# Filling a two-layer gated MLP kernel: where weights are loaded, decoded and where the first convolutions are summed

## Chip, cores and metric

One NeuronCore of a Trainium2 chip. The metric is the device time of one execution, in microseconds. The profile is one execution taken by the hardware profiler; every "row" below is from it.

## What is computed

Inputs are `x` (2 x 4096 x 192), `weight_gen` (2 x 4096 x 8 x 7) and four weight matrices that reach the kernel as 64-bit floats (drawn as float64). The result is 8192 x 192.

```python
w = softmax(weight_gen, axis=-1)                      # 8 heads, 7 taps
x1[b, s, h*24 + g] = sum_k w[b, s, h, k] * x_pad[b, s + k, h*24 + g]   # causal, 6 zeros ahead
x2 = (sigmoid(x1 @ w_gate) * (x1 @ w_val)) @ w_out1   # 192 -> 1536 -> 192
h  = x2 @ w_in2                                       # 192 -> 2048
out = (h * cos(h)) @ w_out2                           # 2048 -> 192
```

## The kernel before

**Tiling.** 8192 tokens are 128 partitions x 64 token columns; a chunk `c` is TC = 4 of those columns, so 512 tokens, and there are NCH = 16 chunks. Every operand of a matmul is split into a high and a low part in fp32r (`split`, line 117: ACT copies the high part, POOL subtracts to get the low part), and three of the four products are summed. Contraction runs over 64 rows, two row halves side by side, so matmuls come in pairs "64x512".

**Steps.** A `Step` (line 505) is one column block of a layer. A layer-1 step has 18 `ph` matmuls (`hidden`, line 422), then on ACT a sigmoid (`gate`, line 527), on DVE the product (`product1`, line 530), on ACT and POOL the two halves `gh` and `gl` (`halves`, lines 565 and 566), and later 10 `po` matmuls (`out_matmuls`, line 437) that sum the output. Layer 1 has 12 steps per chunk. Layer 2 has 8 steps of two blocks each, with a reduction, a Sin and a product in place of the sigmoid.

**Order.** All steps stand in one list (`segments`, line 593): layer 1 of chunks 0 and 1 first, then layer 2 of chunk 0, layer 1 of chunk 2, layer 2 of chunk 1, and so on. I call layer 1 of chunks 0 and 1 the *fill*: steps 0 to 11 and 12 to 23. The order on each engine is written out by hand. Work that belongs to a later step (softmax, taps, weight decode) stands in a list `side` with a due step, and `do_side` (line 614) emits it ahead of that step's matmuls. Each engine runs its instructions in that order.

**Weights.** A weight piece (`Unit`, line 123, and `OutUnit`, line 148) is DMA'd from the SP queue as two 32-bit words per element and decoded to fp32 (`decode`, line 99): ACT scales the high word (line 106) and the low word (line 107), DVE joins them (line 109), DVE puts the sign back (line 113). Layer-2 input pieces are then scaled on ACT (line 141). Then `split` makes the halves: ACT at line 118, POOL at line 120 or 172. There are 18 pieces: 2 of 384 and 16 of 768 elements a partition (`u` names gate/value or layer-2 input, `o` names output weights). In emission order the split of a piece (line 118) stands ahead of the next step's sigmoid.

**Convolution.** Seven taps (`pr`, `acc`). For chunk 0 each product (DVE half of the heads, POOL half) is transposed by TensorE into the same PSUM banks (line 332), which sums them. For chunks 1 and 2 DVE takes 6 of 8 heads and POOL 2, multiplying and adding into `acc` (lines 268, 282, 292); from chunk 3 on DVE has all heads. `acc` is then extended by a copy (line 313) and transposed in two batches of 12 matmuls (`transpose_tiles`, line 369), with `po` matmuls behind each; ACT copies the high parts (line 400), DVE subtracts to the low parts (line 403), 384 wide, into all slots of `xT`. `first_input` (line 405) does the same for chunk 0 in ten pairs of copy and subtract (lines 416, 417). For layer 2, `finish1` (line 461) fills one slot and a half itself and the others with three SBUF-to-SBUF DMAs.

**Queues.** All DMAs are issued by SP. There are eight completion semaphores; a DMA issue waits until the earlier DMA on its semaphore has landed.

Of the kernel before, what the change touches and what calls it, by code (L numbers as in the profile page):

```python
# [29 lines left out]
def dyn_conv_glu_cos_mlp(  # L30
# [15 lines left out]
    P = 128  # L46
# [15 lines left out]
    NS = NQ + 1  # L62
# [59 lines left out]
    class Unit:  # L122
# [13 lines left out]
        def ops(self):  # L136
# [11 lines left out]
    class OutUnit:  # L148
# [15 lines left out]
        def ops(self):  # L164
# [3 lines left out]
            self.t = wpool.tile([P, JG, 2 * D], F32R, name="outu", tag=self.name)  # L168
            f = f.rearrange("p (j d) -> p j d", j=JG)
# [33 lines left out]
    def load_group(g, tiles, tag):  # L203
# [3 lines left out]
        nc.sync.dma_start(  # L207
# [32 lines left out]
    def load_x(c):  # L240
# [8 lines left out]
        if h:  # L249
            for b in range(B):  # L250
                p0 = b * per_batch
                nc.sync.dma_start(
# [393 lines left out]
    with tc.manual_schedule():  # L646
# [53 lines left out]
        for _ in s0:  # L700
            pass
# [138 lines left out]
```

## Time and profile before

| what | value |
|---|---|
| median of 3 runs | 1293.6 us (1292.59 to 1294.15) |
| profiled execution | 1293.17 us |
| its span, first to last instruction | 1291.4 us |
| PE busy in the span | 1236.2 us (96%), 10984 matmuls |
| DVE, ACT, POOL busy | 942.7, 810.9, 736.6 us |
| mean granted TensorE clock | 0.975 of full |

The span is 1.8 us shorter than the execution's time. PE is busy 96% of the whole, but that is a mean over unlike parts: the first 160 us differ from the rest, so the stretches have to be read one at a time. Busy time on PE includes time at half clock, which the granted clock tells (1.0 is 2.4 GHz, 0.5 is 1.2 GHz).

### The profile page before, as it was taken

The page shows a single profiled execution, that of the slowest core. Times are in us where ns is not written, and L with a number is a line of the kernel's source. Part 1 is how long each engine was busy: PE and PEld are TensorE (multiplying, and loading weights), DVE is VectorE, ACT ScalarE, POOL GpSimd, SP SyncE. Part 2 cuts the span into 40 slices and gives each one's busy share as a digit, 9 for nine tenths or more (in the row PEclk, how much of TensorE's full clock was granted, in tenths as well). Part 3 has the DMA queues.
Part 4 walks back from the last instruction along what each step waited for, and adds up shares of the span by engine and source line. Part 5 has one row for each costly group of instructions (what it writes and reads, how often), then busy time and mean ns, then how long its engine had stood idle before and what let it go on. Part 6 is the DMA issues. An engine that isn't in the chain of part 4 may idle for free.

```text
span 1291.4 us, 26697 instructions
## 1 busy us (share of the span) xinstructions
PE 1236.2 (96%) x10984; PEld 1037.2 (80%) x10984; DVE 942.7 (73%) x1323; ACT 810.9 (63%) x1345; POOL 736.6 (57%) x563
## 2 busy tenths in 40 slices
PE   6687799999999999999999999999999999999997
PEld 4465688888888888888888888888888888888885
DVE  6979688777778677777867777786776768673585
ACT  5564584756748475674847567484756748475675
POOL 5778664554646455474746547374654737464473
PEclk7788899999999999999999999999999999999999
DMA  9951010100111100011110001111000111010010
GB/s 213 184 122 55 1 37 13 53 28 32 26 44 26 55 17 22 32 25 44 26 54 18 22 31 26 44 25 48 21 18 32 26 44 26 13 26 14 1 26 26
DMA packets 21066, 51.51 MB, mean 40 GB/s; under 512 B 1876, under 2 KB 6482, under 8 KB 20944
## 3 DMA queue, kind: packets, MB, share of 16 engines
q1 hardware_dynamic: 20944, 49.80, 15.2%
q8 instruction: 86, 1.41, 0.5%
q14 instruction: 36, 0.29, 0.1%
HBM read 30.92 MB, written 6.29 MB: 29 GB/s over the span
## 4 chain that ended last, share of the span: by engine, by line
PE 75%; DVE 6%; ACT 2%; issue 1%; POOL 0%; DVEq 0%; ACTq 0%
PE ph L430 41%; PE po L449 33%; DVE acc L292 2%; DVE wk L530 1%; ACT wk L527 1%; PE pt L377 1%; DVE wk L538 1%; ACT gh L565 1%; DVE va L459 1%; DVE wk L546 1%; DVE wk L555 0%; DVE wk L541 0%; ACT wk L551 0%; POOL gl L566 0%; PE pf L490 0%
## 5 line engine op out<-in xcount | busy, mean ns | idle before, releaser
L566 POOL TENSOR_TENSOR gl<-wk,gh 128x512 fp32r<-128x512 f32 x446 | 606.5, 1365 | 507.2 <-ACT gh L565 385.2
L430 PE MATMUL ph<-xT,unit 64*128 64x512 f32 x5760 | 781.8, 393 | 20.4 <-ACT wk L527 11.0
L430 PEld LDWEIGHTS ph<-xT,unit 64*128 64x128 f32 x5760 | 612.2, 187 | 128.9 <-ACT wk L527 13.6
L449 PE MATMUL po<-gh,outu 64*128 64x512 f32 x2688 | 565.3, 394 | 16.3 <-ACT outu L118 6.4
L449 PE MATMUL po<-gl,outu 64*128 64x512 f32 x1792 | 473.3, 390 | 2.9 <-POOL gl L566 2.8
L449 PEld LDWEIGHTS po<-gh,outu 64*128 64x128 f32 x2688 | 408.4, 186 | 70.2 <-DVE va L459 10.8
L565 ACT ACTIVATE gh<-wk 128x512 fp32r<-128x512 f32 (+1 forms) x450 | 282.8, 629 | 272.4 <-DVE wk L530 216.7
L449 PEld LDWEIGHTS po<-gl,outu 64*128 64x128 f32 x1792 | 324.7, 186 | 34.4 <-POOL gl L566 4.2
L530 DVE TENSOR_TENSOR wk<-ph,wk 128x512 f32<-128x512 f32 x192 | 131.7, 686 | 153.7 <-ACT wk L527 144.7
L555 DVE SCALAR_TENSOR_TENSOR wk<-ph,wk 128x512 f32<-128x512 f32 (+1 forms) x258 | 166.9, 686 | 39.7 <-ACT wk L551 39.7
L551 ACT ACTIVATE wk<-wk,sin_bias 128x512 f32<-128x512 f32 (+1 forms) x258 | 171.4, 714 | 9.7 <-DVE wk L541 3.3
L527 ACT ACTIVATE wk<-ph 128x512 f32<-128x512 f32 x192 | 113.8, 593 | 50.4 <-PE ph L430 49.4
L538 DVE TENSOR_SCALAR wk<-ph 128x512 f32<-128x512 f32 x129 | 87.9, 682 | 66.9 <-PE ph L430 63.6
L292 DVE TENSOR_TENSOR acc<-acc,pr 128x768 f32<-128x768 f32 (+1 forms) x90 | 123.3, 1370 | 0.4
L545 ACT ACTIVATE wk<-ph 128x512 int32<-128x512 f32 x129 | 75.7, 587 | 74.5 <-PE ph L430 73.8
L282 DVE TENSOR_TENSOR pr<-xp,sm 128x768 f32<-128x768 f32 (+1 forms) x90 | 103.2, 1147 | 0.1
L541 DVE SCALAR_TENSOR_TENSOR wk<-wk,ph 128x512 f32<-128x512 f32 x129 | 88.1, 683 | 4.4
L546 DVE TENSOR_TENSOR wk<-wk,ph 128x512 f32<-128x512 int32 x129 | 87.3, 677 | 0.0
L459 DVE TENSOR_TENSOR va<-po,va 128x512 f32<-128x512 f32 x32 | 22.0, 687 | 34.6 <-PE po L449 32.5
L403 DVE TENSOR_TENSOR xT<-pt,xT 128x384 fp32r<-128x384 f32 x60 | 30.6, 552 | 18.1 <-ACT xT L400 18.1
L400 ACT ACTIVATE xT<-pt 128x384 fp32r<-128x384 f32 x60 | 26.2, 488 | 16.6 <-PE pt L377 16.6
L120 POOL TENSOR_TENSOR unit<-wf,unit 128x768 fp32r<-128x768 f32 (+1 forms) x11 | 21.1, 1917 | 19.3 <-ACT unit L118 19.3
(66 smaller groups left out, 566.5 us busy)
## 6 DMA issues: line engine op xcount, KB each, us to landing
xp<-in_x_dram SPq DMA_DIRECT2D x14, 960.0 KB, 4.7
xT<-xT SPq DMA_DIRECT2D x48, 256.0 KB, 3.3
out_dram<-o SPq DMA_DIRECT2D x16, 384.0 KB, 2.3
rawo<-in_moe_w_out_dram SPq DMA_DIRECT2D x7, 768.0 KB, 21.3
raw<-in_moe_w_in_dram SPq DMA_DIRECT2D x8, 384.0 KB, 20.7
raw<-in_moe_w_gate_dram SPq DMA_DIRECT2D x5, 384.0 KB, 15.2
raw<-in_moe_w_val_dram SPq DMA_DIRECT2D x5, 384.0 KB, 15.6
sm<-in_weight_gen_dram SPq DMA_DIRECT2D x5, 336.0 KB, 5.1
```

What stands on the lines that cost most here:

```text
L282: eng.tensor_tensor(out=pr.rearrange("p t (h g) -> p t h g", g=G), in0=xt[:, k:k + TC, a * G:b * G].rearrange("p t (h g) -> p t h g", g=G) ...
L292: eng.tensor_tensor(out=acc[:, :, c], in0=acc[:, :, c], in1=pr, op=ALU.add)
L430: nc.tensor.matmul(ps[i], lhsT=u.t[i * HP:(i + 1) * HP, w, q, c0:c0 + P], rhs=tokens(xt, x, i, q), start=n == 0, stop=n == len(terms) - 1,)
L449: nc.tensor.matmul(po[2 * i + a], lhsT=w[r, d0:d0 + P], rhs=g[r], start=first and g is gh and d0 < D, stop=last and g is gl,)
L527: nc.scalar.activation(out=self.w[0], in_=self.ps[0], func=AF.Sigmoid)
L530: nc.vector.tensor_tensor(out=self.w[0], in0=self.ps[1], in1=self.w[0], op=ALU.mult)
L538: nc.vector.tensor_scalar(out=w, in0=u, scalar1=0.25, scalar2=ROUND_MAGIC, op0=ALU.add, op1=ALU.add)
L546: nc.vector.tensor_tensor(out=w, in0=w.bitcast(I32), in1=u, op=ALU.subtract)
L551: nc.scalar.activation(out=w, in_=w, func=AF.Sin, scale=-SIN_SCALE, bias=sin_bias)
L555: nc.vector.scalar_tensor_tensor(out=w, in0=self.ps[i][:, r], scalar=TWO_PI, in1=w, op0=ALU.mult, op1=ALU.mult)
L565: nc.scalar.activation(out=gh, in_=w, func=AF.Copy)
L566: eng.tensor_tensor(out=gl, in0=w, in1=gh.bitcast(F32), op=ALU.subtract)
```

## The change

- Weight loads: the gate part of a piece goes by SP, the value part by ACT's DMA queue, from the first piece to the last of layer 1; softmax weights and one of the two history blocks of chunk 0's input go by ACT too. The history of chunk 1's input is copied on POOL from chunk 0's tile.
- Decode: ACT uses Prelu with a scale and a slope instead of Copy, so that the sign bit comes out of the shift; the second DVE operation (line 113) is gone.
- A piece's split is put in a list `late` and emitted behind the step's sigmoid, not ahead of it.
- Decodes have new due steps; layer 2's eight DVE decodes all stand at steps 13 to 22.
- Convolutions of chunks 0, 1, 2: DVE multiplies all heads, nothing is added on DVE or POOL, TensorE transposes all seven products into the same banks (16 matmuls each, 8 of them 64 columns of weights wide). One or four warm-up matmuls follow each tap of chunk 0. Chunk 1's input is made one step earlier (AHEAD = 2).
- First two steps: their high-part products are issued ahead of the low-part ones (`mm_high`).
- Inputs of chunks 2 to 15: one batch of 16 transposes; ACT and DVE fill one slot and a half, and three DMAs copy the other slots (`exchange`), as for layer 2.

The diff, cut:

```diff
     def decode(raw, f):
-        nc.scalar.activation(out=f, in_=raw[:, :, 1].bitcast(F32), func=AF.Copy, scale=2.0**-112)
+        nc.scalar.activation(
+            out=f, in_=raw[:, :, 1].bitcast(F32), func=AF.Prelu, scale=2.0**-112, alpha=2.0**32
+        )
         nc.scalar.activation(out=low, in_=low, func=AF.Copy, scale=LOW_SCALE)
         yield
         nc.vector.scalar_tensor_tensor(
             out=fi, in0=fi, scalar=3, in1=low, op0=ALU.logical_shift_left, op1=ALU.bitwise_or
         )
-        yield
-        nc.vector.scalar_tensor_tensor(
-            out=fi, in0=raw[:, :, 1], scalar=1 << 31, in1=fi, op0=ALU.bitwise_and, op1=ALU.bitwise_or
-        )
...
+            late.append(lambda: self.halves(f))
...
-        if h:
+        if c == 1:
+            nc.gpsimd.tensor_copy(out=t[:, 0:h, :], in_=xp[0][:, TC:TC + h, :])
+        elif h:
             for b in range(B):
                 p0 = b * per_batch
-                nc.sync.dma_start(
+                queues[b % 2].dma_start(
...
+    def conv_products(c):
+        big = tpool.tile([P, K - 3, TC, D], F32, name="prs", tag="xA" if c % 2 == 0 else "xB")
+        att[c] = [big[:, k] for k in range(K - 3)] + [product_tile(), product_tile(), acc_tile()]
+        for k, pr in enumerate(att[c]):
+            tap(c, k, pr)
+            yield
...
+    def transposes(p, src, first, end):
+        blocks = [(0, 0)] + [(2, t) for t in range(TC)] + [(0, t) for t in range(1, TC)]
...
+    def split_input(xt, p, fast):
+        for slot in (OWN[0], OTHER[0], OWN[1]) if fast else OWN:
+            high(nc.scalar, xt, p, slot)
+        yield
+        if fast:
+            for slot in OTHER[1:]:
+                high(nc.vector, xt, p, slot)
+        for slot in (OWN[0], *OTHER[:2], OWN[1], OTHER[2]) if fast else OWN:
+            low(xt, p, slot)
+        if not fast:
+            exchange(xt)
...
-        todo += [(s2 + u.j0 - 3, u) for u in units2] + [(s2 + o.j0 // 2, o) for o in outs2]
+        todo[n1:] = [(seg_start[1, 1] + 1 + i * (J1 - 1) // 8, u) for i, (_, u) in enumerate(todo[n1:])]
...
+        for k, _ in enumerate(first_input()):
+            if k in (3, 5):
+                next(decoding)
+                run(late)
+            if k == 2:
+                units1[3].load(act, 1)
+                units1[4].load(act, 1)
+            if k == K:
+                units1[5].load(act, 1)
+                units1[6].load(sp, 0)
+                units1[6].load(act, 1)
+                outs1[2].load(sp)
+            else:
+                warm_up(1 if k < K - 1 else 4)
+        for st in steps[:2]:
+            st.mm_high()
...
                 st.gate()
+                run(late)
                 pending.append(st.product1)
```

How the order of instructions moves, at three places. First ACT in step 17 of the fill, the decode of a layer-2 piece. Names: `raw` loaded words, `wf` decoded piece, `unit` its high half, `wk` the sigmoid's output, `gh` the high half of the step's result. Before (the like place, ahead of the sigmoid of step 19):

```order
L565 ACTIVATE gh<-wk 128x512 [waits DVE_49]
L106 ACTIVATE wf<-rawo 128x768 [waits DMAHW7_49]
L107 ACTIVATE rawo<-rawo 128x768
L141 ACTIVATE wf<-wf 128x768 [waits DVE_49]
L118 ACTIVATE unit<-wf 128x768 [waits Activation_49]
L527 ACTIVATE wk<-ph 128x512 [waits PE_49,Pool_49]
L565 ACTIVATE gh<-wk 128x512 [waits DVE_49]
```

After:

```order
L547 ACTIVATE gh<-wk 128x512 [waits DVE_49]
L146 ACTIVATE wf<-wf 128x768 [waits DVE_49]
L109 ACTIVATE wf<-rawo 128x768 [waits DMAHW5_49,Activation_49]
L112 ACTIVATE rawo<-rawo 128x768
L509 ACTIVATE wk<-ph 128x512 [waits PE_49]
L119 ACTIVATE unit<-wf 128x768 [waits Activation_49]
L547 ACTIVATE gh<-wk 128x512 [waits DVE_49]
```

The split of the piece (L118, now L119) has moved from ahead of the sigmoid to behind it.

Second, ACT from the transposed first input on, after the change; before, the loads stood on SP and row L106 followed the copies of `xT` directly:

```order
L349 ACTIVATE xT<-pt 64x4x64 x4
L136 DMA raw<-in_moe_w_val_dram 64x3x512 [waits DMAHW4_49]
L136 DMA raw<-in_moe_w_val_dram 64x3x512 [waits DMAHW6_49]
L109 ACTIVATE wf<-rawo 128x768 [waits DMAHW2_49,Pool_49]
L112 ACTIVATE rawo<-rawo 128x768
L509 ACTIVATE wk<-ph 128x512 [waits PE_49]
L119 ACTIVATE unit<-wf 128x768 [waits DVE_49,Activation_49]
```

Two DMA issues now stand on ACT between the input's copies and the decode of the first output piece; the second waits for the semaphore that piece 4's gate part signals. A like pair stands on ACT ahead of the first decode (L109, 128x384), waiting for the value part of piece 0 and the gate part of piece 2.

Third, PE at the input of a later chunk, before:

```order
L377 MATMUL pt<-ident,acc 128x64 x12
L449 MATMUL po_2165<-gh,outu 128x512
L449 MATMUL po_2167<-gh,outu 128x512
L449 MATMUL po_2165<-gh,outu 128x512
L449 MATMUL po_2167<-gh,outu 128x512
L449 MATMUL po_2165<-gl,outu 128x512
L449 MATMUL po_2167<-gl,outu 128x512
L449 MATMUL po_2166<-gh,outu 128x512
L449 MATMUL po_2168<-gh,outu 128x512
L449 MATMUL po_2166<-gl,outu 128x512
L449 MATMUL po_2168<-gl,outu 128x512
L377 MATMUL pt<-ident,acc 128x64 x12
```

After, with `po` rows before and behind:

```order
L426 MATMUL po_2287<-gl,outu 128x512
L426 MATMUL po_2289<-gl,outu 128x512
L328 MATMUL pt<-ident,acc 128x64 x2
L328 MATMUL pt<-ident,acc 64x64 x8
L328 MATMUL pt<-ident,acc 128x64 x6
L426 MATMUL po_2286<-gh,outu 128x512
L426 MATMUL po_2288<-gh,outu 128x512
```

24 transposes in two batches have become 16 in one, half of them with 64 weight columns.

## Rows read from the trace of the kernel before

**Rows 1.** Busy time by stretch: stretch, length, then PE PEld DVE ACT POOL, clock.
```profile
41.58:92.26 50.68, 40.40 (x278) 30.40 (x274) 43.28 (x39) 30.96 (x47) 41.74 (x32) 0.80 0.83 163
92.26:158.80 66.54, 51.93 (x360) 39.35 (x362) 52.52 (x45) 33.50 (x53) 47.87 (x40) 0.87 0.09 27
230.00:305.00 75.00, 74.73 (x684) 64.12 (x682) 57.02 (x82) 47.72 (x81) 42.17 (x32) 1.00 0.11 33
```
**Rows 2.** PE in order of time, start of the fill: start, us, line, operation, idle before.
```profile
24.53 8.13 PE L430 MATMUL ph<-xT,unit 64*128 64x512 f32 x53 [2.74 <-ACT xT L416]
36.15 0.79 PE L449 MATMUL po<-gh,outu 64*128 64x512 f32 x2 [3.48 <-ACT outu L118]
39.71 0.79 PE L449 MATMUL po<-gh,outu 64*128 64x512 f32 x2 [2.77 <-POOL outu L172]
41.58 3.89 PE L430 MATMUL ph<-xT,unit 64*128 64x512 f32 x18
```
**Rows 3.** ACT in order of time, one step with a decode.
```profile
124.81 0.63 ACT L565 ACTIVATE gh<-wk 128x512 fp32r<-128x512 f32 x1 [0.76 <-DVE wk L530]
125.34 0.93 ACT L106 ACTIVATE wf<-rawo 128x768 f32<-128x768 f32 x1
126.18 0.92 ACT L107 ACTIVATE rawo<-rawo 128x768 uint32<-128x768 uint32 x1
127.66 0.84 ACT L141 ACTIVATE wf<-wf 128x768 f32<-128x768 f32 x1 [0.57 <-DVE wf L113]
128.54 0.84 ACT L118 ACTIVATE unit<-wf 128x768 fp32r<-128x768 f32 x1
129.29 0.58 ACT L527 ACTIVATE wk<-ph 128x512 f32<-128x512 f32 x1
130.62 0.63 ACT L565 ACTIVATE gh<-wk 128x512 fp32r<-128x512 f32 x1 [0.76 <-DVE wk L530]
```
**Rows 4.** Groups by line and shape, 24.5 to 158.8 us: busy, mean ns | idle before.
```profile
L566 POOL TENSOR_TENSOR gl<-wk,gh 128x512 fp32r<-128x512 f32 x24 | 37.0, 1542 | 10.0 <-ACT gh L565 8.8 <-DMA raw<-in_moe_w_in_dram 0.9
L292 DVE TENSOR_TENSOR acc<-acc,pr 128x576 f32<-128x576 f32 x12 | 21.3, 1778 | 0.0
L120 POOL TENSOR_TENSOR unit<-wf,unit 128x768 fp32r<-128x768 f32 x9 | 19.0, 2115 | 11.5 <-ACT unit L118 11.5
L282 DVE TENSOR_TENSOR pr<-xp,sm 128x576 f32<-128x576 f32 x12 | 16.7, 1399 | 0.1
L530 DVE TENSOR_TENSOR wk<-ph,wk 128x512 f32<-128x512 f32 x24 | 16.4, 685 | 20.5 <-ACT wk L527 20.4 <-issue 0.2
L113 DVE SCALAR_TENSOR_TENSOR wf<-raw,wf 128x768 uint32<-128x768 uint32 x9 | 13.1, 1457 | 0.2
```
**Rows 5.** SP's DMA issues in order of time (start, us).
```profile
14.51 0.59 SPq L131 DMA_DIRECT2D raw<-in_moe_w_gate_dram  x1
30.40 9.22 SPq L131 DMA_DIRECT2D raw<-in_moe_w_in_dram  x4
```
**Rows 6.** PE in order of time, a later step and the two transpose batches.
```profile
300.10 2.42 PE L430 MATMUL ph<-xT,unit 64*128 64x512 f32 x18
302.14 0.84 PE L449 MATMUL po<-gh,outu 64*128 64x512 f32 x4
303.28 2.42 PE L430 MATMUL ph<-xT,unit 64*128 64x512 f32 x18
...
306.46 0.56 PE L377 MATMUL pt<-ident,acc 64*128 64x64 f32 x9
...
308.08 0.53 PE L377 MATMUL pt<-ident,acc 64*128 64x64 f32 x9
```
**Rows 7.** PE, two products of chunk 0's convolution transposed.
```profile
11.45 2.25 PE L332 MATMUL pt<-ident,pr 64*128 64x64 f32 x32 [0.44 <-POOL pr L342]
```
**Rows 8.** Busy time by stretch, as rows 1, around that.
```profile
10.00:20.00 10.00, 7.39 (x112) 6.19 (x112) 6.83 (x9) 3.69 (x7) 7.81 (x8) 0.55 1.10 243
```
**Rows 9.** Groups on ACT and DVE, 8 to 26 us: the first input's copies and subtracts.
```profile
L416 ACT ACTIVATE xT<-pt 64x256 fp32r<-64x256 f32 x8 | 2.9, 378 | 0.7 <-DVE xT L417 0.4
L417 DVE TENSOR_TENSOR xT<-pt,xT 64x256 fp32r<-64x256 f32 x8 | 3.0, 419 | 0.4
```

More of the change, by code (lines that the diff above doesn't have):

```diff
@@ L296, in conv_ops @@
         last = None
-        for k in range(1, K):
+        for k in range(1, K + 1):
             yield
-            pr = [product(k, sh) for sh in shares]
+            if k < K:
+                pr = product_tile()
+                tap(c, k, pr)
+                if last is not None:
+                    yield
             if last is not None:
-                yield
-                for p, sh in zip(last, shares):
-                    add(p, *sh)
+                nc.vector.tensor_tensor(out=acc, in0=acc, in1=last, op=ALU.add)
@@ L304, in conv_ops @@
             last = pr
[L305 to L313 removed]
+    def conv_products(c):
+        big = tpool.tile([P, K - 3, TC, D], F32, name="prs", tag="xA" if c % 2 == 0 else "xB")
+        att[c] = [big[:, k] for k in range(K - 3)] + [product_tile(), product_tile(), acc_tile()]
+        for k, pr in enumerate(att[c]):
+            tap(c, k, pr)
+            yield
@@ L420, in tokens @@
-    def tokens(xt, x, half, q):
-        return xt[half * HP:(half + 1) * HP, x, (q - half) % NQ, :]
+    def transposes(p, src, first, end):
+        blocks = [(0, 0)] + [(2, t) for t in range(TC)] + [(0, t) for t in range(1, TC)]
+        for q, t in blocks:
+            for h in range(2):
+                r = slice(h * HP, (h + 1) * HP)
+                nc.tensor.matmul(
+                    p[h][0:min(P, D - q * HP), (2 * q + t) * HP:(2 * q + t + 1) * HP],
+                    lhsT=src[r, t, q * HP:min(D, q * HP + P)], rhs=ident[r, r], is_transpose=True,
+                    start=first and (q, t) == blocks[0], stop=end and (q, t) == blocks[-1],
+                )
@@ L508, in __init__, with mm_high @@
             self.u, self.c0, self.tiles = (map1 if layer == 1 else map2)[j]
+        ps = None
+        def mm_high(self):
+            self.more = hidden(self.u, self.c0, xT[self.layer, self.c])
+            self.ps = next(self.more)
         def mm_hidden(self):
-            self.ps = hidden(self.u, self.c0, xT[self.layer, self.c])
+            if not self.ps:
+                self.mm_high()
+            next(self.more)
         def runs(self):
@@ L635, in chain, with warm_up, run @@
             yield
-            next(g, None)
-            yield
     def cost(n):
         return 0.06 + 1.05e-3 * n
-    def shares(c):
-        h = HEADS[c] if c < len(HEADS) else H
-        return [e for e in ((nc.vector, 0, h), (nc.gpsimd, h, H)) if e[1] < e[2]]
+    def warm_up(n):
+        for _ in range(n):
+            ps = ps_h.tile([P, N], F32, name="pw", tag="h")
+            nc.tensor.matmul(ps[:, 0:P], lhsT=ident, rhs=ident, start=True, stop=True)
+    def run(ops):
+        for f in ops:
+            f()
+        ops.clear()
@@ L666, in dyn_conv_glu_cos_mlp @@
-        while todo[0] not in units2:
-            todo.pop(0).load(nc.sync)
+        for due, u in todo:
+            add_side(seg_start[1, 1] if u in units2 or u in outs2 else 0, due, [2.4], decoding)
+        todo = [u for _, u in todo if u in units2 or u in outs2]
         s0, s1 = softmax_ops(0), softmax_ops(1)
```

299 lines of the change are left out of this document (116 added, 183 removed).

## The prediction, made before the changed kernel was run

> **What bounds the kernel now.** I read busy time by stretch first, because the 96% of PE hides where time is lost. From 230 to 305 us, one of the repeating 75.00 us rounds (layer 2 of a chunk and layer 1 of another), PE is busy 74.73 us at full clock [rows 1]: there only fewer PE instructions help. The fill is different. Steps 3 to 11 take 50.68 us and steps 12 to 23 take 66.54 us [rows 1], while a layer-1 step costs PE 3.18 us where nothing waits: from one group of 18 `ph` matmuls to the next, 2.04 us for them and 1.14 us for ten `po` [rows 6]. Nine steps are 28.6 us, twelve are 38.2 us. So the two stretches lose about 22 and 28 us, partly in waits and partly at half clock (0.80 and 0.87).
>
> The second view was PE in order of time. The first steps' matmuls start at 24.53 us, then PE waits 3.48 us for the ACT half of the first output piece and 2.77 us for its POOL half, so that step 3 starts at 41.58 us [rows 2].
>
> Third, what a step in the second stretch waits for. ACT runs `gh`, two decode copies, the scale, the piece's split, and only then the sigmoid; from one `gh` to the next it is 5.81 us [rows 3]. The split stands ahead of the sigmoid, and cannot start before DVE's second decode operation. DVE in turn waits 20.4 us in the fill for sigmoids ahead of its products [rows 4]. It is a loop through two engines, and PE stands behind it.
>
> **The sum.** It is made against the profiled execution, 1293.2 us, which is 0.4 us under the median.
>
> *Start to step 3 (now 41.58 us).* The input's split becomes six ACT copies and four DVE copies side by side instead of ten copy-subtract pairs in turn. At 0.38 us for a copy and 0.42 us for a subtract [rows 9], the high parts are ready after about 2.3 us, and the high products of two steps cover the ten subtracts (4.2 us). That is worth some 2 us. But ACT now issues DMAs with waits. Two stand ahead of the first decode; the later of them needs piece 2's gate part, whose landing freed SP at 14.51 us before [rows 5]. Two stand ahead of the first output piece's decode; the later needs piece 4's gate part, which landed by 30.40 us [rows 5]. The dropped history loads may bring this forward by about 2 us. ACT would come to that place near 24 us and be held until about 29 us; then two decode copies (1.85 us) and the sigmoid (0.58 us) end at about 31.5 us, the rest of the chain (`unit`, `gh`, two copies, sigmoid, `outu`: 0.84 + 0.63 + 1.85 + 0.58 + 0.84 = 4.7 us [rows 3]) at 36.2 us, POOL's low half 2.1 us later [rows 4], and the ten `po` another 1.1 us: 39.5 us, 40 us with a slower clock. I take **-1.5 us**. Not held at all it would be some 2.5 us better still (-4); held longer than I think, or with PE waiting behind its added warm-ups, +2.5.
>
> *Steps 3 to 11 (now 50.68 us).* Engine sums with the change. PE: nine steps 28.6 us, and 112 transposes in place of 24. Sixteen took 1.13 us [rows 7] at a clock of 0.55 [rows 8]; at full clock half of that, 0.57 us, so seven products take 4.0 us. PE 32.6 us. ACT: nine sigmoids and `gh` 10.9, five pieces at 1.85 + 0.84 = 13.5, six input copies 2.3: 26.7 us. DVE: nine products 6.2, five decode operations at 1.46 [rows 4] 7.3, seven taps, input copies and subtracts 14 x 0.42 = 5.9. A tap of all heads is 768 wide; 576 wide took 1.40 us beside POOL [rows 4], so between that and 1.87; I take 1.6, the added POOL shares being gone: 11.2. DVE 30.6 us, against 43.3 us busy before [rows 1]. POOL: nine `gl` at 1.54, five pieces at about 2.1 [rows 4]: 24.4 us, before 41.7. So the adds (1.78 us each) and second decode operations leave, and PE becomes the longest. Part of this stretch still follows a wait of PE: 7 us at half clock cost 3.5 us. 36.1 us, and a tenth for waits in order: 39.5 us, **-11.2 us**. Bounds: 36 us without waits (-14.7), 46 us where half of the old loss stays (-4.7).
>
> *Steps 12 to 23 (now 66.54 us).* PE 38.2 + 4.0 = 42.2 us. ACT: 14.5 for sigmoids and `gh`, eight splits 6.7, seven pairs of decode copies 13.0, four scales 3.4, five operations of chunk 0's layer-1 end at a sigmoid's 0.58, 2.9, four input copies 1.5: 42.0 us. POOL: twelve `gl` 18.5, eight pieces 16.8, three operations of that end at the same 1.54, 4.6: 40 us. DVE: 8.2 + 11.7 + 11.2 + some 3 = 34 us, before 52.5. All eight layer-2 pieces are now joined in this stretch. With the split behind the sigmoid a step with a decode takes ACT 0.63 + 1.85 + 0.58 + 0.84 = 3.9 us, and with a scale 4.7 us and a wait of about 0.8 us for DVE. Before, the stretch was 1.27 times its busiest engine (66.54 over DVE's 52.52). The same ratio gives 53.6 us: I take 54, **-12.5 us**. Bounds: 47 us (ratio 1.1, -19.5) and 60 us (-6.5).
>
> *Inputs of chunks 3 to 15.* Two batches of 12 transposes cost PE this much: from the first to the second 1.62 us pass, of which ten `po` take 1.14, so 0.48 us a batch [rows 6], 0.96 us an input. One batch of 16 is 0.57 us by rows 7, 0.64 if the narrower ones save nothing. I take 0.38 us an input, times 13, **-5.0 us**; bounds -2.6 and -7.8. The three DMAs cost no engine time but SP's: the slots are read a layer-2 segment later, eight steps of at least 18 + 20 matmuls, over 34 us, and the like three DMAs of layer 2 already have less. If that cover were gone, the first step of a segment would wait for a landing. ACT's copy of 256 and some 0.4 us of DVE subtracts go too, and are worth nothing where PE is full. One input copy on POOL (chunk 1's history) lies in POOL's idle time.
>
> Sum: -1.5 - 11.2 - 12.5 - 5.0 = -30.2 us. **1263 us.**
>
> **Rivals.** (a) *Transposes cool the clock.* In the stretch of the first transposes the granted clock was 0.55, although PE was busy 7.39 of 10 us with them [rows 8]; but it had also been idle before, so the row does not tell the two apart. With 112 transposes in one run at the ends of steps 10 and 23, the clock would fall to 1.2 GHz: 4.0 us more for each run if it all ran so, and about a step's 3.18 us lost in the matmuls behind. Two such places, at between 2 and 7.2 us each, cost about 9 us: 1272 us. The Trainium skill's page "TensorE: Matmul & The Clock Gate", section "Part 4: PE-mode transpose", says that transposes do not count as activity that lifts the clock; by that rule this rival holds, and the 0.55 agrees without proving it.
>
> (b) *ACT's order takes over.* The loop through ACT and DVE is broken, but ACT carries the same copies and now nine DMA issues, six of them behind landings. If the steps with a decode stay near 5 us and step 3 starts no earlier, the fill gains only some 12 us (0, -4.7 and about -7): 1276 us with the later inputs' 5 us, 1281 us without; 1278 us. For it: ACT and PE sums are equal in steps 12 to 23. Against: in the old loop ACT was busy 33.5 of 66.5 us, so it was not full but waiting.
>
> (c) *Slower: the one batch makes PE wait at each input.* Both transposed banks come back only after four ACT copies (1.5 us) and four subtracts (1.7 us), behind a product of 0.69 us: 3.9 us. Meanwhile PE has two `po` groups, a hidden group and one more `po` group: 2.28 + 2.04 + 1.14 = 5.5 us. The kernel gets slower only where the wait per input passes (25.2 + 5.0)/13 = 2.3 us, so where that chain takes 7.8 us, twice its sum. At a wait of 3 us: 1293.2 - 25.2 + 39 = 1307 us. DVE's last tap operations stand one step ahead, which speaks for it; the slack of 1.6 us speaks against.
>
> (d) *The later transposes do not get cheaper.* The batch is bound by something else and PE's round stays at 75.00 us: 1268 us. It can be read at once in any later round.
>
> **Chances.** The forecast (fill -25, later inputs -5, within some 9 us) 0.62; (a) 0.14; (b) 0.16; (d) 0.04; (c) 0.04. All bounds together would reach from 1247 to 1282 us; they will not all fall one way, so the range is 1251 to 1280 us, which leaves out (c), the upper end of (b) and the best tail of the forecast. A measurement of this kernel tells about 0.2% from no change, 2.6 us. Faster by more than that 0.94, within 0.02, slower 0.04.
>
> **What would show it.** Step 3 starts near 40 us, step 12 near 79 us, layer 2 of chunk 0 near 133 us instead of 158.8 us. In steps 13 to 22 the sigmoid follows its `ph` matmuls at once, and DVE's wait for sigmoids falls below half of 20.4 us. A later round takes 74.6 us with PE still over 99% busy. ACT is idle behind a DMA landing ahead of the first output piece's decode, around 24 to 29 us. The prediction is wrong if layer 2 of chunk 0 starts after 146 us, if a later round is not shorter than 75.0 us, or if PE shows a new wait behind the input's subtracts; a clock below 0.8 between 75 and 85 us would speak for (a).

## The result, and the profile after the change

| | before | after |
|---|---|---|
| median of 4 runs | 1293.21 us (1292.59 to 1294.15) | 1271.12 us (1269.66 to 1272.69) |
| ratio, 95% interval | | 0.9829 [0.9812, 0.9846] |
| profiled execution, its span | 1293.17, 1291.4 us | 1270.46, 1268.6 us |

The change gains 22 us; 30 were forecast. The span of the profiled execution became 22.8 us shorter. Four stretches of the changed kernel (start to step 3, steps 3 to 11, steps 12 to 23, a later piece of 75 us; columns as in [rows 1]):

```profile
24.66:42.89 18.23, 11.94 (x65) 7.36 (x66) 12.67 (x25) 10.91 (x17) 7.46 (x5) 0.81 1.08 224
42.89:82.64 39.75, 35.27 (x367) 30.13 (x363) 31.62 (x36) 23.34 (x39) 29.96 (x18) 0.96 0.92 190
82.64:140.21 57.57, 49.53 (x449) 40.25 (x451) 38.19 (x35) 38.53 (x60) 42.45 (x28) 0.91 0.11 32
215.21:290.21 75.00, 74.75 (x678) 65.54 (x676) 56.15 (x83) 46.61 (x79) 41.81 (x31) 1.00 0.15 41
```

Against [rows 1, 2]: step 3 starts at 42.89 us instead of 41.58 (+1.3), steps 3 to 11 take 39.75 us instead of 50.68 (-10.9), steps 12 to 23 take 57.57 us instead of 66.54 (-9.0). The rest gained 4.2 us.

**Start.** ACT in order of time (start, us; the bracket is the idle time before):

```profile
23.25 2.00 ACT L349 ACTIVATE xT<-pt 128x256 fp32r<-128x256 f32 x6 [2.04 <-PE pt L328]
29.84 2.54 ACTq L136 DMA_DIRECT2D raw<-in_moe_w_val_dram  x2
32.49 0.89 ACT L109 ACTIVATE wf<-rawo 128x768 f32<-128x768 f32 x1 [7.24 <-DMA raw<-in_moe_w_gate_dram]
34.04 0.58 ACT L509 ACTIVATE wk<-ph 128x512 f32<-128x512 f32 x1
34.52 0.84 ACT L119 ACTIVATE unit<-wf 128x768 fp32r<-128x768 f32 x1
```

and PE behind it:

```profile
35.41 1.65 PE L407 MATMUL ph<-xT,unit 64*128 64x512 f32 x6 [3.68 <-ACT unit L119]
37.97 2.93 PE L407 MATMUL ph<-xT,unit 64*128 64x512 f32 x12 [0.91 <-POOL unit L121]
41.86 0.51 PE L426 MATMUL po<-gh,outu 64*128 64x512 f32 x2 [0.56 <-POOL outu L183]
```

From 25.25 us ACT does nothing, and then its two DMA issues (line 136), the second at 31.79 us, last until 32.4 us. The sigmoid and `unit` half behind them cost PE 3.68 us.

**Steps 12 to 23.** The three largest waits of PE behind the input of step 12:

```profile
104.45 0.51 PE L426 MATMUL po<-gl,outu 64*128 64x512 f32 x2 [3.66 <-POOL gl L548]
...
118.72 3.44 PE L407 MATMUL ph<-xT,unit 64*128 64x512 f32 x17 [2.00 <-DVE wk L512]
123.03 4.31 PE L407 MATMUL ph<-xT,unit 64*128 64x512 f32 x18 [0.86 <-ACT wk L509]
```

DVE, and POOL at the same time:

```profile
109.95 1.17 DVE L114 SCALAR_TENSOR_TENSOR wf<-wf,rawo 128x768 uint32<-128x768 uint32 x1
111.03 7.03 DVE L276 TENSOR_TENSOR prs<-xp,sm 128x768 f32<-128x768 f32 x1
117.99 0.68 DVE L512 TENSOR_TENSOR wk<-ph,wk 128x512 f32<-128x512 f32 x1
```
```profile
104.36 2.69 POOL L183 TENSOR_TENSOR outu<-wf,outu 128x256 fp32r<-128x256 f32 x2
107.02 2.00 POOL L121 TENSOR_TENSOR xT<-va,xT 128x512 fp32r<-128x512 f32 x1
...
112.24 1.27 POOL L548 TENSOR_TENSOR gl<-wk,gh 128x512 fp32r<-128x512 f32 x1
113.48 1.84 POOL L121 TENSOR_TENSOR unit<-wf,unit 128x768 fp32r<-128x768 f32 x1
115.28 1.29 POOL L548 TENSOR_TENSOR gl<-wk,gh 128x512 fp32r<-128x512 f32 x1
116.53 2.67 POOL L183 TENSOR_TENSOR outu<-wf,outu 128x256 fp32r<-128x256 f32 x2
```

POOL works without a gap from 98.0 to 119.2 us. One tap of DVE takes 7.03 us (another, at 123.62 us, 0.95 us), and the product behind it is what PE waits 2.00 us for. This one tap is worth little by itself: kernel 2 below has the same order on every engine from step 12 on, and in its trace no tap there takes more than 2.61 us (a decode operation beside the same run of POOL takes 4.31 us); its steps 12 to 23 take 56.66 us by PE's rows, 0.9 us less.

**Later rounds.** The same operation of one round, twelve rounds apart; first before, then after:

```profile
242.12 0.59 ACT L458 ACTIVATE va<-po 128x512 f32<-128x512 f32 x1
...
1142.33 0.59 ACT L458 ACTIVATE va<-po 128x512 f32<-128x512 f32 x1
```
```profile
223.27 0.59 ACT L435 ACTIVATE va<-po 128x512 f32<-128x512 f32 x1
...
1119.21 0.59 ACT L435 ACTIVATE va<-po 128x512 f32<-128x512 f32 x1
```

900.21 / 12 = 75.02 us a round before, 895.94 / 12 = 74.66 us after: 0.36 us less, where 0.38 was forecast. Twelve rounds as busy time by stretch, before and after:

```profile
230.00:1130.20 900.20, 896.99 (x8164) 758.51 (x8162) 659.48 (x949) 574.18 (x958) 499.20 (x373) 1.00 0.10 30
```
```profile
230.00:1126.00 896.00, 892.81 (x8068) 772.49 (x8066) 651.00 (x949) 563.11 (x945) 498.83 (x372) 1.00 0.15 41
```

PE runs 96 instructions fewer, eight a round, and is busy 4.18 us less; its idle time is the same (3.2 us). The gain there is in PE's work and not in its waits.

### The profile page after: what moved, and what is told of

Read it like the earlier page. It is cut to its first block, busy times and chain, and to the rows that moved or that the text cites. A ratio compares the mean times of both kernels' runs of the same rounds, so it can differ in the third digit from the quotient of the medians.

```text
span 1268.6 us, 26949 instructions
## 1 busy us (share of the span) xinstructions
PE 1230.6 (97%) x11076; PEld 1051.6 (83%) x11076; DVE 902.2 (71%) x1307; ACT 795.2 (63%) x1328; POOL 710.8 (56%) x529
## 4 chain that ended last, share of the span: by engine, by line
PE 71%; DVE 7%; ACT 5%; issue 2%; POOL 0%; DVEq 0%; ACTq 0%
PE ph L407 39%; PE po L426 31%; DVE acc L302 2%; DVE wk L512 1%; ACT L533 1%; ACT wk L509 1%; ACT wk L533 1%; ACT gh L547 1%; DVE wk L537 1%; DVE wk L520 1%; DVE va L436 1%; ACT wk L527 1%; PE pt L328 1%; DVE wk L528 1%; DVE wk L523 0%
## 5 line engine op out<-in xcount | busy, mean ns | idle before, releaser
L407 PEld LDWEIGHTS ph<-xT,unit 64*128 64x128 f32 x5760 | 615.6, 186 | 113.9 <-DVE wk L512 10.5
L426 PE MATMUL po<-gh,outu 64*128 64x512 f32 x2688 | 557.2, 390 | 4.7 <-ACT gh L547 1.8
L426 PEld LDWEIGHTS po<-gl,outu 64*128 64x128 f32 x1792 | 321.2, 184 | 32.0 <-POOL gl L548 6.1
L276 DVE TENSOR_TENSOR pr<-xp,sm 128x768 f32<-128x768 f32 x89 | 101.0, 1137 | 2.2 <-PE pt L328 1.2
L302 DVE TENSOR_TENSOR acc<-acc,pr 128x768 f32<-128x768 f32 x78 | 100.9, 1294 | 0.4
L355 DVE TENSOR_TENSOR xT<-pt,xT 64x256 fp32r<-64x256 f32 (+1 forms) x76 | 27.3, 414 | 21.5 <-ACT xT L349 21.3
L349 ACT ACTIVATE xT<-pt 64x256 fp32r<-64x256 f32 (+1 forms) x68 | 20.5, 377 | 23.4 <-PE pt L328 23.3
```

The costliest lines, as they stand in the source:

```text
L276: nc.vector.tensor_tensor(out=out.rearrange("p t (h g) -> p t h g", g=G), in0=xp[c][:, k:k + TC, :].rearrange("p t (h g) -> p t h g", g=G) ...
L302: nc.vector.tensor_tensor(out=acc, in0=acc, in1=last, op=ALU.add)
L407: nc.tensor.matmul(ps[i], lhsT=u.t[r, w, (s + i) % NQ, c0:c0 + P], rhs=xt[r, x, s, :], start=n == 0, stop=n == len(terms) - 1,)
L426: nc.tensor.matmul(po[2 * i + a], lhsT=w[r, d0:d0 + P], rhs=g[r], start=first and g is gh and d0 < D, stop=last and g is gl,)
```

## The experiments

Each median is of four executions; ratios are to the kernel before. Two more marks come from each profile: `va` 0 and `va` 1, when ACT begins to sum the output of layer 1 of chunk 0 and of chunk 1. The second less the first stands for the length of steps 12 to 23: 56.66 us for the changed kernel, where PE's rows give 57.57 us, and 66.94 us before, where they give 66.54 us.

| kernel | median us | ratio, 95% interval | `va` 0 | `va` 1 | difference |
|---|---|---|---|---|---|
| before | 1293.2 | 1 | 99.17 | 166.11 | 66.94 |
| after | 1271.1 | 0.9829 [0.9812, 0.9846] | 90.93 | 147.59 | 56.66 |
| 1 late value loads on SP | 1266.3 | 0.9796 [0.9781, 0.9811] | 87.84 | 143.23 | 55.39 |
| 2 no warm-up between taps | 1271.3 | 0.9835 [0.9816, 0.9854] | 90.32 | 146.11 | 55.79 |
| 3 split ahead of sigmoid | 1271.6 | 0.9840 [0.9823, 0.9856] | 92.01 | 149.01 | 57.00 |
| 4 DVE adds | 1275.7 | 0.9866 [0.9851, 0.9881] | 94.89 | 151.81 | 56.92 |
| 5 second decode operation | 1287.0 | 0.9956 [0.9941, 0.9971] | 98.67 | 161.65 | 62.98 |
| 6 no exchange | 1304.3 | 1.0083 [1.0068, 1.0098] | 93.85 | 151.85 | 58.00 |
| 7 two pieces later | 1272.2 | 0.9835 [0.9820, 0.9850] | 90.78 | 143.81 | 53.03 |
| 8 end of layer 1 on DVE | 1272.1 | 0.9841 [0.9825, 0.9858] | 90.65 | 146.02 | 55.37 |
| 9 = 1 + early join | 1262.8 | 0.9761 [0.9746, 0.9775] | 85.35 | 140.71 | 55.36 |
| 10 = 9 + lows on DVE | 1263.3 | 0.9767 [0.9751, 0.9783] | 85.46 | 139.86 | 54.40 |
| 11 = 10 + scale in sums | 1258.3 | 0.9727 [0.9711, 0.9744] | 85.31 | 136.15 | 50.84 |
| 12 = 11 + copies behind sigmoid | 1261.8 | 0.9756 [0.9741, 0.9770] | 84.10 | 137.88 | 53.78 |

The marks are of one execution each. Kernel 6 has the instructions of the changed kernel up to the input made in step 23, and still a `va` 0 that is 2.9 us later: smaller differences of a mark say little alone.

**1. Late value loads on SP.**
```diff
-                units1[5].load(act, 1)
+                units1[5].load(sp, 1)
                 units1[6].load(sp, 0)
-                units1[6].load(act, 1)
+                units1[6].load(sp, 1)
```


> The value parts of pieces 5 and 6 are issued by SP instead of ACT; the rest is the changed kernel. Theory A (ACT is held by its own DMA issues): in the changed kernel ACT idles from 25.25 us and its two issues end at 32.4 us, and the decode of the first output piece starts right behind them. Without them that decode starts up to 7 us earlier; the chain behind it (decode copies, outu halves, po) moves with it, so step 3 starts 2 to 3 us before 42.89 us and the whole takes about 1268.5 us. Rival B (the transfers set it): the first output piece or piece 3 has not landed by then, because the DMA engines are over 90% busy from 5 us on; ACT then waits for a landing in the same place, step 3 stays within 1 us of 42.9 us and the time at 1271 us. Rival C: SP, now held by the waits of these two issues, starts the layer-2 loads late and the fill loses 1 to 2 us.

Theory A holds, at nearly twice its size: 4.9 us less than after, where 2.6 were expected. ACT in the same place:

```profile
21.96 2.00 ACT L349 ACTIVATE xT<-pt 128x256 fp32r<-128x256 f32 x6 [1.09 <-PE pt L328]
24.58 0.89 ACT L109 ACTIVATE wf<-rawo 128x768 f32<-128x768 f32 x1 [0.63 <-DMA rawo<-in_moe_w_out_dram]
```

The piece had landed by 24.58 us. It had in the changed kernel too, where an issue of SP that waits for this landing starts at 24.39 us; ACT came to it at 32.49 us only because of its own issues. Step 3 starts at 39.43 us, 3.5 us earlier. SP's later start of the layer-2 loads cost nothing that shows.

**2. No warm-up between taps.**
```diff
-                warm_up(1 if k < K - 1 else 4)
+                warm_up(0 if k < K - 1 else 4)
```


> The six single warm-up matmuls between the taps of chunk 0 are left out; the eight before and the four after the last tap stay. Theory A (warm-ups lengthen the first input): each tap costs PE 1.04 us of transposes and 0.72 us of warm-up at half clock, so the first hidden matmuls, at 24.66 us, start 2 to 4 us earlier; but as ACT holds the first output piece's decode until 32.4 us, step 3 moves by less than 1 us and the time stays within 1.5 us of 1271 us. Rival B (they buy the clock): without them the granted clock rises later than 24.3 us, the first 24 hidden matmuls run at half clock longer, step 3 starts 1 to 3 us later and the time is 1272 to 1274 us.

The time is the same, as A said, but not for its reason: the first hidden matmuls start 0.6 us earlier, not 2 to 4, since PE then waits 2.89 and 1.04 us for DVE's taps. The warm-ups fill time in which PE would wait for DVE anyway.

**3. Split ahead of the sigmoid.**
```diff
-            late.append(lambda: self.halves(f))
+            self.halves(f)
```
(and the same for output pieces)

> One part undone: a piece's split stands again ahead of the next sigmoid, right behind DVE's decode operation; all else as in the changed kernel. Theory A (the loop ACT split, ACT sigmoid, DVE product, DVE decode was the old bound): steps 3 to 23, now 97.3 us, get 8 to 14 us longer, and the time is 1279 to 1285 us. Rival B (the loop was broken by DVE's lighter work, not by the order): with one decode operation and no adds DVE is early enough, and the time stays within 3 us of 1271 us.

Rival B: no difference that can be told. The part of the change that was to break the loop is worth nothing by itself, but not because it does nothing. PE's waits from 24.5 to 141 us (total us, times, longest), in this kernel:

```profile
PE ph L407 <- ACT wk L509: 10.1, 6, 4.0
```

and in the changed kernel:

```profile
PE ph L407 <- ACT unit L119: 3.7, 1, 3.7
PE ph L407 <- POOL unit L121: 3.0, 2, 2.1
PE ph L407 <- ACT wk L509: 1.1, 2, 0.9
```

With the split ahead PE waits for sigmoids and for no `unit` half; with the split behind it is mostly the other way round. The new place trades one wait for the other.

**4. DVE adds for chunks 1 and 2.**
```diff
-                n, ops = K, conv_products(c)
+                n, ops = 2 * K, conv_ops(c)
```
(and two operations at each due step of chunk 1's taps)


> One part undone: for chunks 1 and 2 DVE adds the seven products itself, and TensorE transposes one sum (16 matmuls) instead of seven products (112); one batch and the late split stay. Theory A (DVE's adds were a large part of the old fill): twelve adds of 1.3 to 1.8 us come back, about 10 us in each of steps 3 to 11 and 12 to 23; PE gets 3.4 us shorter in each. As PE is the longest of steps 3 to 11 and DVE has 16 us spare there, that stretch moves by -2 to +2 us; steps 12 to 23, where DVE taps are stretched by POOL, by +2 to +8 us: 1272 to 1280 us. Rival B (transposes are as dear as the adds): both stretches get 2 to 4 us shorter, 1264 to 1268 us. Rival C (transposes cool the clock): the half-clock stretches at 61.8 to 65.2 and 106 to 127 us vanish as well, 1262 us.

4.6 us slower, in A's range, but not in A's place: `va` 0 is 4.0 us later and steps 12 to 23 are as long as after. In that stretch the adds and the 96 transposes weigh the same.

**5. The second decode operation.**
```diff
-            out=f, in_=raw[:, :, 1].bitcast(F32), func=AF.Prelu, scale=2.0**-112, alpha=2.0**32
+            out=f, in_=raw[:, :, 1].bitcast(F32), func=AF.Copy, scale=2.0**-112
...
+        nc.vector.scalar_tensor_tensor(
+            out=fi, in0=raw[:, :, 1], scalar=1 << 31, in1=fi, op0=ALU.bitwise_and, op1=ALU.bitwise_or
+        )
```


> One part undone: the second DVE operation of a decode is back (ACT scales with Copy, DVE joins and then puts the sign), all else as changed. Theory A (DVE has room since the adds are gone): 16 operations of about 1 to 1.5 us; in steps 3 to 11 DVE is busy 23.3 of 39.8 us and hides its five; in steps 12 to 23, eight more, 9 to 12 us of DVE work beside POOL, cost 3 to 6 us: 1274 to 1277 us. Rival B (still in the loop): each adds its whole duration to a step with a decode, 13 x 1.2 = 16 us: 1285 us or more. Rival C: hidden everywhere, 1271 us.

Rival B: 15.8 us slower, 72% of what the change gained (15.8 of 22.1). DVE and then ACT in a step with a decode:

```profile
101.09 0.95 DVE L114 SCALAR_TENSOR_TENSOR wf<-wf,raw 128x768 uint32<-128x768 uint32 x1
102.07 1.99 DVE L117 SCALAR_TENSOR_TENSOR wf<-raw,wf 128x768 uint32<-128x768 uint32 x1
```
```profile
104.09 0.85 ACT L149 ACTIVATE wf<-wf 128x768 f32<-128x768 f32 x1 [2.20 <-DVE wf L117]
```

ACT idles 2.20 us for the second operation, and its decode copies and sigmoid stand behind. In the whole fill ACT waits 19.8 us for it (9.5 ahead of scales, 10.3 ahead of splits); in the changed kernel it waits 2.2 us in such places. The loop of the prediction is real, and what its breaking was worth lies in DVE's part of it: with one operation the place of the split costs nothing (experiment 3). Whether the place would count with two was not run.

**6. No exchange.**
```diff
-        yield from split_input(xt, p, c < LEAD)
+        yield from split_input(xt, p, True)
```


> One part undone: all inputs of layer 1 are written to every slot by ACT and DVE (three slots more copies and subtracts), with no DMA copies; the single batch of 16 transposes stays. Theory A (the later rounds gained 0.36 us each by eight fewer transposes alone): PE is full in a round and the copies lie beside it, so a round stays at 74.66 us and the time at 1271 us, within 1.5 us. Rival B (the shorter drain of the transposed banks is what gained): a round goes back to about 75.0 us and the time to 1275 us. Rival C: with the longer drain PE waits at each input for a free bank, 0.5 to 1.5 us in 13 rounds, 1278 to 1290 us.

Rival C, beyond its range: 33 us slower than after, 11 us slower than before. A round takes 76.91 us (ACT's sum at 229.74 us to the one at 1152.67, over 12), 2.25 us more; 13 such rounds make 29 of the 33 us. Chunk 4's input, on ACT, DVE and PE:

```profile
294.94 1.97 ACT L349 ACTIVATE xT<-pt 128x256 fp32r<-128x256 f32 x6 [1.17 <-PE pt L328]
```
```profile
296.68 1.54 DVE L351 CAST xT<-pt 64x256 fp32r<-64x256 f32 x4 [2.12 <-ACT xT L349]
298.25 3.84 DVE L355 TENSOR_TENSOR xT<-pt,xT 128x256 fp32r<-128x256 f32 x10
```
```profile
301.91 2.65 PE L407 MATMUL ph<-xT,unit 64*128 64x512 f32 x18 [1.40 <-DVE xT L355]
```

The two transposed banks are in use until the last subtract, 7.1 us after the first copy, and the next step's matmuls need a bank. PE has this wait in each of the twelve rounds, 1.40 us every time; the rest of the 2.25 us is time in which PE counts as busy, and was not followed up.

**7. Two pieces later.**
```diff
-        todo[n1:] = [(seg_start[1, 1] + 1 + i * (J1 - 1) // 8, u) for i, (_, u) in enumerate(todo[n1:])]
+        todo[n1:] = [(seg_start[1, 1] + due, u) for due, (_, u) in zip([1, 2, 3, 5, 6, 8, 14, 17], todo[n1:])]
```


> The last two output pieces of layer 2 are decoded inside layer 2 of chunk 0 (two and five steps into it) instead of at steps 21 and 22. Theory A (steps 12 to 23 are bound by the sum of small work in order): the stretch, now 57.6 us against 42.5 us of ACT, loses two pieces of about 2.5 us of ACT each and gets 4 to 7 us shorter; layer 2 of chunk 0 gives 1 to 3 us of it back because its steps of 4.3 us have only about 1 us of ACT spare; the whole 1267 to 1269 us. Rival B: only the part at steps 13 to 17 is short of an engine (POOL), the end of the stretch has slack, so nothing is gained there and layer 2 loses 2 to 4 us: 1273 to 1275 us.

Both were half right: steps 12 to 23 get 3.6 us shorter, and layer 2 of chunk 0 gives all of it back; at its end both kernels are at the same time (182.39 and 182.38 us).

**8. The end of chunk 0's layer 1 on DVE.**
```diff
+        eng = nc.gpsimd if c else nc.vector
-        nc.gpsimd.tensor_tensor(out=vc[0:HP, :], in0=vc[0:HP, :], in1=vs, op=ALU.add)
+        eng.tensor_tensor(out=vc[0:HP, :], in0=vc[0:HP, :], in1=vs, op=ALU.add)
```
(and both low halves behind it on `eng`)

> The three POOL operations of the end of chunk 0's layer 1 (an add and two low halves, about 6 us of POOL at steps 13 to 16) go to DVE, for chunk 0 alone. Theory A (POOL's unbroken run from 100.5 to 119.2 us stretches the DVE tap to 7.03 us and sets the 3.66 us and 2.00 us waits of PE): POOL gets done 4 to 6 us earlier, the tap falls to 1 to 3 us, steps 12 to 23 get 3 to 6 us shorter, and the time is 1265 to 1268 us. Rival B (ACT's order sets the stretch): ACT's operations and their order are the same, so the stretch stays within 1 us of 57.6 us. Rival C: DVE, which already has the decode joins and taps, is late with the sigmoid products; the stretch gets longer by 1 to 3 us.

The waits that A named are gone, the gain is not there. The longest tap is 2.61 us and no `po` waits for `gl`, but a new wait takes its place:

```profile
98.35 1.74 DVE L447 TENSOR_TENSOR vc<-vc,vs 64x512 f32<-64x512 f32 x1 [4.33 <-ACT vs L445]
```
```profile
100.74 4.21 PE L407 MATMUL ph<-xT,unit 64*128 64x512 f32 x17 [3.26 <-DVE wk L513]
```

The add waits 4.33 us for ACT, and a product for which PE waits stands behind it on DVE.

**9. Early join.**
```diff
+            if n in (2, 3):
+                yield
...
+            if k == K - 1:
+                next(decoding)
             if k == K:
+                run(late)
+                next(decoding)
```


> On top of the run with the late value loads on SP: piece 2's decode on DVE stands ahead of the first input's ten subtracts, its split right behind the input copies, and the first output piece's decode operation ahead of the first sigmoid product. Theory A (the loads gone, step 3 is set by DVE's order): with the loads on SP, piece 2 is joined only at 29.22 us, behind the subtracts, and PE waits 1.55 us for its low half and 1.14 us for the output piece's; now both are ready 2 to 4 us earlier, step 3 starts 2 to 4 us earlier, the time falls from 1266.3 to about 1263 us. Rival B (the transfers are next): the third or fourth piece has not landed, ACT waits for it ahead of the sigmoids and nothing is gained: 1266 us. Rival C: the gain at step 3 is spent by steps 3 to 11, which then wait for pieces that land late: 1265 to 1267 us.

A, to 0.2 us. Step 3 starts at 36.23 us.

**10. The two lows alone on DVE.** As 8, with the add left on POOL.
```diff
+        eng = nc.gpsimd if c else nc.vector
...
-        split(xt[:, 0, 0, :], xt[:, 1, 0, :], va)
+        split(xt[:, 0, 0, :], xt[:, 1, 0, :], va, eng)
...
-        split(xt[0:HP, 0, 2, :], xt[0:HP, 1, 2, :], vc[0:HP, :])
+        split(xt[0:HP, 0, 2, :], xt[0:HP, 1, 2, :], vc[0:HP, :], eng)
```

> The kernel of the early join, and the two low halves at the end of chunk 0's layer 1 on DVE instead of POOL (the add stays on POOL). Theory A (POOL's unbroken run stretches the DVE tap and makes PE wait 3.7 us for gl; with all three operations on DVE the tap was 2.6 us and that wait was gone, but the add on DVE stood 4.33 us behind ACT ahead of a product, for which PE then waited 3.26 us): with the add left on POOL neither wait is there, steps 12 to 23 are 3 to 5 us shorter, and the time is 3 to 5 us below that of the early join alone. Rival B: ACT's order takes the place, and the time is within 1 us of it.

Rival B: the same time as 9. PE's waits there are again for `gl` (2.96 us) and for two sigmoids (1.06 and 1.18 us).

**11. The scale in the sums.**
```diff
-            if self.scale:
-                nc.scalar.activation(out=f, in_=f, func=AF.Copy, scale=self.scale)
...
-            nc.scalar.activation(out=v, in_=po[i], func=AF.Copy)
-            nc.vector.tensor_tensor(out=v, in0=po[2 + i], in1=v, op=ALU.add)
+            nc.scalar.activation(out=v, in_=po[i], func=AF.Copy, scale=scale)
+            nc.vector.scalar_tensor_tensor(out=v, in0=po[2 + i], scalar=scale, in1=v, op0=ALU.mult, op1=ALU.add)
```
(`scale` is 1/2pi at layer 1's end, else 1)

> On top of the early join with the lows on DVE: the four scale operations of layer-2 input pieces (0.85 us of ACT each, with a wait of ACT for DVE's join of 0.2 to 0.9 us ahead of each) are gone; the factor stands in the two operations that sum layer 1's output, on ACT and DVE, which are there anyway. Theory A (ACT's order sets steps 12 to 23 by now): in that kernel ACT idles there only behind DVE, and PE's last waits of 0.5 to 1.2 us are for sigmoids that stand behind a scale and two copies; four times 1.0 to 1.5 us, the time falls by 4 to 6 us to about 1258 us. Rival B (POOL and DVE set it, as they share their time): the stretch moves by less than 1 us, 1262 to 1263 us. Later rounds stay at 74.66 us in both.

A, to 0.3 us: 5.0 us less for four operations of 0.85 us. PE's start of step 12 and of layer 2 of chunk 0, in kernel 10 and in 11:

```profile
77.17 2.62 PE L407 MATMUL ph<-xT,unit 64*128 64x512 f32 x18 [1.43 <-DVE xT L355]
...
132.46 2.37 PE L407 MATMUL ph<-xT,unit 64*128 64x512 f32 x18
```
```profile
78.06 2.65 PE L405 MATMUL ph<-xT,unit 64*128 64x512 f32 x18 [1.44 <-DVE xT L353]
...
128.76 2.37 PE L405 MATMUL ph<-xT,unit 64*128 64x512 f32 x18
```

Steps 12 to 23, where the operations were, took 55.29 us and take 50.70 us, 4.6 us less (3.6 by the `va` marks); layer 2 starts 3.7 us earlier, and the two profiled executions differ by 3.5 us (1262.50 and 1258.95), so nothing is gained behind the stretch. PE's waits for sigmoids in it went from 2.6 to 0.4 us. This was done on top of 10, where those waits had grown and the one for `gl` had shrunk; in the changed kernel itself it was not run. This is the fastest kernel here, 12.8 us below after (1271.1 - 1258.3).

**12. Copies behind the sigmoid.**
```diff
...
             if after:
-                next(after)
+                start.append(after)
+                if n < 4:
+                    next(start.pop())
+                else:
+                    late.append(lambda: start and next(start.pop()))
```


> On top of the kernel with the scale in the sums: from piece 4 on, the two decode copies of the next piece stand behind the sigmoid and the split on ACT instead of ahead of the sigmoid. Theory A (what PE waits for is the sigmoid, since it frees the hidden banks, while gh has two steps of slack): the sigmoid starts 1.7 us earlier in a step with a decode and PE's waits behind sigmoid and product go; another 2 to 4 us below the kernel with the scale in the sums. Rival B (the sum of ACT's work counts, not its order): within 1 us of it. Rival C: gh, now behind the copies, makes gl and then the output matmuls late: 1 to 4 us slower than it.

3.5 us slower, C's size, by another wait. `gh` is not what PE waits for most; DVE meets POOL again:

```profile
91.29 5.21 DVE L274 TENSOR_TENSOR prs<-xp,sm 128x768 f32<-128x768 f32 x1
```
```profile
97.75 3.64 PE L405 MATMUL ph<-xT,unit 64*128 64x512 f32 x16 [2.76 <-DVE wk L511]
```

The new order shifted a tap into a run of POOL; in 11 the tap of that place took 2.62 us. PE's waits for products in steps 12 to 23 are 6.1 us, against 0.5 in 11. How much of the 3.5 us is this stays open.

## Why the prediction was right, and where it was off

The sign and the range were right; the forecast was 8 us too low (1263 against 1271). Of the 7.4 us by which the span's gain fell short (22.8 of 30.2), 2.8 lie in the start and 3.5 in steps 12 to 23. By its terms:

- **Start to step 3: -1.5 forecast, +1.3 measured.** The mechanism was right, the size wrong, and with it the sign of the term. "Held until about 29 us" was 32.4 us: the step took some 2 us off the landing at 30.40 us [rows 5] because history loads are dropped, and the issue that waits for that landing went out at 31.79 us instead, 1.4 us later than before. The chain behind it took 10.5 us to step 3, as in the sum (29 to 39.5 us). Experiment 1 prices the hold at 4.9 us of the whole. The bound "+2.5" held.
- **Steps 3 to 11: -11.2 forecast, -10.9 measured.** Right as a sum: PE, the longest, was busy 35.27 us where 36.1 were forecast, and waited the rest. Of the change's parts, the adds are worth 4.0 us and the decode operation 7.7 us at `va` 0 (experiments 4 and 5); the split's place 1.1 us, too little to tell from one trace.
- **Steps 12 to 23: -12.5 forecast, -9.0 measured.** This is the step that failed most. It sized the stretch as 1.27 times its busiest engine, with PE's 42.2 us at full clock; it was 1.36 times that. ACT's sum was near (42.0 forecast, 38.53 busy). PE was busy 49.53 us, partly at half clock: by the mean of 0.91 some 10 of the 57.57 us are at half clock, which costs about 5 us (an estimate from that row), and the sum names no term for it here. And the engines' operations stand in one order: ACT's copies, scale and sigmoid have DVE's join between them, so work taken from ACT came back in full, 3.4 us of scales for 3.6 to 4.6 us of stretch, by the mark taken (experiment 11, on top of 10). That is rival (b)'s mechanism, in this stretch alone; (b) as a whole was not what happened, as steps 3 to 11 gained what was forecast. The second thing the ratio hid is POOL's unbroken run, which makes `gl` late and DVE's operations long; the one tap of 7.03 us is at most 1 us of it (kernel 2). In the changed kernel itself PE's waits there are 4.4 us for `gl`, 2.2 for products and 1.1 for sigmoids. Removing POOL's run without a new wait was not achieved (experiments 8 and 10).
- **"With the split behind the sigmoid."** The prediction counted this among the things that break the loop. Undone alone it costs nothing (experiment 3), and DVE's wait for sigmoids went from 20.4 to 20.0 us, not "below half": DVE got lighter and waits where it worked. With the split ahead, in experiment 3, it is 30.0 us. The sign that I named for the loop was a bad one; PE's wait for sigmoids in the fill tells more, 11.0 us before and 1.1 us after, although experiment 3 shows most of that coming back as other waits.
- **Later inputs: -5.0 forecast, about 13 x 0.36 = 4.6 measured.** Right, by fewer transposes: over twelve rounds PE's busy time fell by 4.18 of the 4.2 us.

The rivals. **(a)** fell, although its time, 1272 us, was nearer to the result than the forecast: that is chance, as its mechanism is not there. Stretches of the two runs of 112 transposes, columns as in [rows 1]:

```profile
71.39:75.46 4.07, 3.55 (x115) 3.34 (x113) 1.37 (x3) 1.12 (x2) 3.13 (x3) 1.00 1.03 372
134.47:137.96 3.49, 3.49 (x117) 3.49 (x114) 0.39 (x1) 0.00 (x0) 2.82 (x3) 1.00 0.02 5
```

The clock stays granted at 1.00, 2.4 GHz, in both, and from 75 to 85 us, where below 0.8 was to speak for (a), it is 1.00 too; 4.0 us of PE were forecast and 4.1 and 3.5 us passed. In the second run sixteen transposes take 0.50 us, against 1.13 us at a clock of 0.55 [rows 7, 8]. By the rule of the Trainium skill, "TensorE: Matmul & The Clock Gate", section "Part 4: PE-mode transpose", that transposes do not count as TensorE being busy in the same way, one would expect the clock to fall, if the rule holds for a clock that is already up; here, behind busy matmuls, it did not. Longer runs of transposes were not made. (The row of the clock needs care before 24 us: it gives 1.00 in the changed kernel, while sixteen transposes take 1.04 us there.) **(c)** did not happen in the later rounds: the copies and subtracts forecast at 3.2 us took 2.4 us (chunk 4's input, from ACT's first copy at 288.46 us to DVE's last subtract at 290.82 us), and PE has no wait behind a subtract there. The sign that the prediction named against itself, a new wait behind the input's subtracts, did come up once, ahead of step 12, whose input ACT and DVE write to all slots:

```profile
82.64 2.65 PE L407 MATMUL ph<-xT,unit 64*128 64x512 f32 x18 [1.44 <-DVE xT L355]
```

Experiment 6 shows what the same wait does at every input. (c)'s condition was a chain of 7.8 us or a wait of 2.3 us an input. With every slot written by ACT and DVE the chain is 7.1 us, a round 2.25 us longer, and the kernel slower than before. The three DMAs, which the prediction priced as costing nothing, are what keeps the single batch of transposes from being a loss. **(d)** fell with the round of 74.66 us. The other sign of being wrong, layer 2 of chunk 0 after 146 us, was not met (140.21 us).

## What to carry to other kernels

A DMA issue that may wait belongs on a queue whose engine has no work behind it: two of them on ACT cost 4.9 us. In a hand-written order, price an operation by what its engine and the next stand waiting for, not by busy sums: one DVE operation per piece was 16 us, four ACT scales were 5 us (on top of another order), and moving an operation behind another was nothing in one place and a loss of 3.5 us in another. When an operation is moved to an idle engine, look first at what will then stand behind its wait.

## What the runs showed of the hardware that was not expected

A DVE tap whose two operands lie in SBUF takes 0.94 to 0.95 us where it starts first or POOL is idle, 1.3 to 2.6 us beside POOL at many places, and 7.03 us at one place of the changed kernel (5.21 in experiment 12). That one ends only after POOL has done a `gl`, a `unit` half and another `gl`, which ran at 1.27, 1.84 and 1.29 us; with DVE getting through, a `gl` takes 1.98 us and a `unit` half 2.49 us. DVE's products, which read PSUM, stay at 0.67 to 0.69 us throughout. A POOL that always has its next operation ready is not enough for this: in the same run without a gap, from 98.0 us on, the taps before took 2.61, 1.26 and 2.04 us. Nor does the order of instructions settle it: kernels 1 and 9 repeat the 7.0 us, while in 2 and 7 it is the decode operation before that tap that is long (4.31 and 4.27 us). What lets DVE in at one place and not at another stays open.

The Trainium skill, "SBUF — State Buffer", section "Who interferes with whom", says that such a DVE instruction contends with a POOL instruction that reads SBUF, that the shared ports are an exclusive lock, and that the order of issue decides who blocks. The trace agrees on who is concerned; that one DVE instruction waits for several of POOL's in turn is more than the page says.
